# Two attention blocks on one core: when VectorE's score tiles may be issued, and how much backlog a projection step may run ahead of

## The chip, the core and the metric

The kernel runs on one core of a Trainium2 chip, as one program. The metric is the time of one execution in microseconds of device time, lower is better. A core has five engines with an instruction stream each: TensorE (in the profile PE, and PEld for its weight loads), VectorE (DVE), ScalarE (ACT), GpSimd (POOL) and SyncE (SP), which here only starts transfers. They meet through semaphores. TensorE writes its results to PSUM, which has eight banks; ScalarE and VectorE take them from there to SBUF.

## The reference

Two blocks read inputs of 2048 x 640 in bf16 and their outputs are set side by side. Block A is softmax attention with 32 heads of 20 columns, block B is linear attention with the same sizes.

```python
def _A_ref(x, wqkv, wo):                       # H = 32, Dh = 20, S = 2048
    qkv = (lambda x, *d: x.transpose(*d))((x @ wqkv).reshape(B, S, 3, H, Dh), 2, 0, 3, 1, 4)
    q, k, v = qkv[0], qkv[1], qkv[2]
    scores = jnp.einsum("bhqd,bhkd->bhqk", q, k) * (Dh ** -0.5)
    p = _softmax(scores, axis=-1)
    o = jnp.einsum("bhqk,bhkd->bhqd", p, v)
    return (lambda x, *d: x.transpose(*d))(o, 0, 2, 1, 3).reshape(B, S, D) @ wo
...
    phi = lambda t: jnp.where(t > 0, t + 1, jnp.exp(t)) + 1e-6     # block B
    pq, pk = phi(q), phi(k)
    kv = jnp.einsum("bhsd,bhse->bhde", pk, v)
    z = jnp.einsum("bhsd->bhd", pk)
    num = jnp.einsum("bhqd,bhde->bhqe", pq, kv)
    den = jnp.einsum("bhqd,bhd->bhq", pq, z)[..., None] + 1e-6
```

## The kernel before

**Work of block A.** The attention is cut into 32 groups n: four stretches of 512 queries (`qc = n // 8`), and in each of them eight groups of four heads (`g = n % 8`). A group has 16 key tiles of 128 keys, and a key tile has four score tiles, one for each head: 128 keys x 512 queries, one PSUM bank. The contraction is short, so four heads' score matmuls can stand in four row strips of TensorE at once; such a burst is called R here. All other matmuls with a narrow output (value products, projections, output projection) are issued as bursts of four column strips, called C.

**Two ways to an exponential.** Most key tiles go to ScalarE: the two score tiles of one R burst fill two banks (`SB`, banks 0 and 1 or 2 and 3), one activation takes both of them to SBUF (`exp_op`, L1740). It writes to the ring `f_PT` of 16 tiles, and four tiles that are there make one value burst. The other key tiles (`DKT` or `DSUB`, chosen by `dset`, L1556) go to VectorE. It scales and clamps one bank at a time to int16 bits of an approximate power (L1644), into one of six slots of `f_Sr`. The key tile is then used three times in a value burst, and between the uses GpSimd adds a constant to all its bits (`add_op`, L1814). So a key tile of VectorE's costs three value bursts, four VectorE instructions and two GpSimd instructions, and one of ScalarE's costs one value burst and two activations. All value bursts of a group add up in one bank, and the next group's can start only when that bank has been read (`norm`, L1818).

**Who decides the order.** The order of all instructions is written when the program is built. The class `_Fast` keeps a clock of its own for each engine with assumed costs, and whenever an engine's clock is the lowest, it picks that engine's next instruction. On the chip the instructions run in the order written, with semaphores where one needs another. For TensorE `try_pe` (L1986) asks in this order:

1. `try_burst` (L1654): the next two score tiles of ScalarE's, if their banks are free, and if Q and K for them are there (`kready`). VectorE's tiles may ride in the strips that are left, in banks 5 to 7.
2. `try_aux`, if a projection or B step has been begun (`self.cur`) and fewer than `PVHI` of ScalarE's finished tiles wait for their value bursts.
3. `try_pv` (L1758): a value burst.
4. `d_burst` (L1707): VectorE's tiles in a burst of their own, if their lead is under `DMIN`.
5. `try_aux` for a new step, and last `filler`, a matmul on zeros.

A projection or B step takes a bank of 5, 6 and 7 too, from its first burst until VectorE has read it. A VectorE tile does so as well (`take_d`, L1626); `dfl` counts those that VectorE has not started yet. The lead is `dlead` (L1649): VectorE tiles issued, less ScalarE tiles issued times the ratio of the two over the whole program. A tile of the next group can be issued ahead, as far as slots, Q and K allow. A ride is wanted if the lead is under `DLEAD` and `dfl` is under `DMAX`; a second one in the same burst if the lead is under `DOUBLE` and `dfl` is still under `DMAX`:

```python
        want = self.dlead() < self.DLEAD and self.dfl < self.DMAX
...
                if self.dlead() < self.DOUBLE and self.abank and self.dfl < self.DMAX:
```

**Order of the whole.** The first two head groups' projections come first, the others are interleaved with attention in a queue (`qa`), strictly in its order: for each chunk of heads Q, then for each of four stretches of keys K and four tiles of V. For the chunks after the first two groups the K and Q pieces go through VectorE to `f_sq` and by small transfers to their strips. Block B's steps (`qb`) start when all K and V are done. The output projection of a stretch of queries comes when its eight groups are done.

Of the kernel before, what the change touches and what calls it, by code (L numbers as in the profile page):

```python
# [750 lines left out]
class _Fast:  # L751
# [7 lines left out]
    DKT = (1, 4, 7, 10, 13)  # L759
    DSUB = (1, 4, 7, 10)  # L760
    NFULL = 4
    NEARLY = 4
    DOUBLE = 2.0
    PH = (0, 42, 89)
    WP = 0.7578125
    STEP = 20.0
    DMIN = 2
    PVHI = 9
    FILL = 0.62
    DMAX = 2  # L770
    DLEAD = 14
    SW = 107.0

    def __init__(self, nc, sch, es, ps, A_x, A_wqkv, A_wo, B_x, B_wqkv, B_wo, out):
# [781 lines left out]
    def dset(self, n):  # L1556
        return self.DKT if n >= self.NEARLY and (n * self.NFULL) % 8 < self.NFULL else self.DSUB

# [95 lines left out]
    def try_burst(self, t):  # L1654
# [18 lines left out]
        post = []  # L1673
        want = self.dlead() < self.DLEAD and self.dfl < self.DMAX
        slack = self.free["act"] - t - 560
        if want:
# [6 lines left out]
            if pd is not None:  # L1683
# [3 lines left out]
                rows.add(pd[1])  # L1687
                if self.dlead() < self.DOUBLE and self.abank and self.dfl < self.DMAX:
                    b = min(self.abank, key=lambda x: self.est("pe", (), (("ps", x),)))
# [296 lines left out]
    def try_pe(self, t):  # L1986
        if self.try_burst(t):
            return True
        if self.cur is not None and self.aexp - 4 * self.apv < self.PVHI and self.try_aux(t):
            return True  # L1990
        if self.try_pv(t):
            return True
        if self.dS < len(self.dq) and self.dlead() < self.DMIN and self.abank and self.d_burst(t):
            return True
# [200 lines left out]
```

## Time and profile before

| | |
|---|---|
| median of 3 runs | 787.47 us (787.3 to 790.4) |
| the profiled execution's own time | 787.67 us |
| its span | 785.5 us |
| TensorE matmul busy | 755.9 us, 96% |
| ScalarE busy | 707.3 us, 90% |
| VectorE busy | 617.7 us, 79% |
| GpSimd busy | 592.5 us, 75% |
| score tiles of ScalarE's | 740 activations of two |
| score tiles of VectorE's | 568 |

The profile is one execution taken by the hardware profiler. It has a page with the busy time of each engine, the costliest groups of instructions and the chain of work that ended last. Further views answer to questions: the timeline lists instructions of an engine in order with the idle time ahead of them in brackets and who ended it; the waits add these up; the table by stretches gives busy time and instruction counts (x) in chosen parts of the span. Matmuls are pipelined, so what a burst costs is read from the start of the next burst and not from its own duration. A matmul group is named by what it reads: `f_Qr,f_KT` are score tiles (one matmul for each tile), `f_PT,f_V` and `f_Sr,f_V` or `f_Sr,f_Vp` are value bursts of four, `f_xT` with a weight is a projection.

### The profile page before, as it was taken

What the parts mean: (1) busy time and instruction counts of PE and PEld (TensorE: products, weight loads), DVE (VectorE), ACT (ScalarE), POOL (GpSimd) and SP (SyncE); (2) the same over time, 40 slices, a digit from 0 to 9 for tenths busy, and PEclk for the clock granted to TensorE, in tenths of its full rate; (3) what the DMA queues carried; (4) which work ended last, traced back from release to release, by engine and by line L of the source; (5) the groups of instructions that cost most, each with busy time, mean ns of one, the idle gap of its engine ahead of it and who ended that gap; (6) DMA issues with size and microseconds to landing.
All of it is one profiled execution on the core that took longest, in us unless ns stands there. A gap on an engine that the chain in (4) does not pass through costs nothing.

```text
span 785.5 us, 25139 instructions
## 1 busy us (share of the span) xinstructions
PE 755.9 (96%) x10960; PEld 266.4 (34%) x10960; DVE 617.7 (79%) x1186; ACT 707.3 (90%) x796; POOL 592.5 (75%) x341
## 2 busy tenths in 40 slices
PE   5999999999989999999999999999999999999996
PEld 2433453234223233333333333323333333233333
DVE  4666759676986778878878787889987798889876
ACT  3479679997999999999999999989999999999990
POOL 6646655787779887787879878777987878787971
PEclk9999999999999999999999999999999999999999
DMA  9000010010520000010200000111000020000002
GB/s 307 17 3 19 19 26 21 22 29 20 129 44 23 23 11 8 14 34 7 40 2 25 30 10 9 50 47 40 23 18 17 33 53 26 20 14 31 6 2 72
DMA packets 38495, 26.34 MB, mean 34 GB/s; under 512 B 21356, under 2 KB 38380, under 8 KB 38380
## 3 DMA queue, kind: packets, MB, share of 16 engines
q1 hardware_dynamic: 35100, 21.81, 10.2%
q10 hardware_dynamic: 3280, 2.87, 1.2%
q8 instruction: 88, 1.44, 0.8%
q14 instruction: 27, 0.22, 0.1%
HBM read 9.58 MB, written 5.24 MB: 19 GB/s over the span
## 4 chain that ended last, share of the span: by engine, by line
PE 53%; ACT 34%; DVE 10%; DMA 1%; issue 1%; SPq 0%; ACTq 0%; DVEq 0%
PE ps L155 53%; ACT f_PT L1740 32%; DVE f_Sr L1644 5%; ACT ps L1277 2%; DMA f_ar<-in_A_wqkv_dram 1%; PE ps L941 1%; DVE f_ar L1387 1%; DMA f_KT<-f_sq 0%; DVE f_T L1840 0%; DVE f_ar L1308 0%; DVE f_OTn L1837 0%; DVE f_ar L1311 0%; DVE f_sq L1158 0%; DVE f_ar L1279 0%; DVE f_sq L1161 0%
## 5 line engine op out<-in xcount | busy, mean ns | idle before, releaser
L1740 ACT ACTIVATE f_PT<-ps 128x1024 bf16<-128x1024 f32 x740 | 694.5, 1101 | 53.4 <-PE ps L155 51.5
L1814 POOL TENSOR_SCALAR f_Sr<-f_Sr 128x2048 int16<-128x2048 int16 x284 | 539.1, 1898 | 134.5 <-PE ps L155 101.7
L1644 DVE TENSOR_SCALAR f_Sr<-ps 128x512 int16<-128x512 f32 x568 | 378.8, 683 | 72.3 <-PE ps L155 68.0
L155 PE MATMUL ps<-f_Qr,f_KT 32*128 32x512 bf16 x2048 | 304.6, 386 | 8.0 <-ACT f_PT L1740 2.9
L155 PEld LDWEIGHTS ps<-f_Qr,f_KT 32*128 32x128 bf16 x2048 | 76.8, 91 | 256.4 <-ACT f_PT L1740 218.7
L155 PE MATMUL ps<-f_ar 128*32 128x320 bf16 (+3 forms) x2496 | 152.1, 311 | 2.8 <-DVE f_Sr L1644 1.0
L155 PE MATMUL ps<-f_PT,f_V 128*21 128x512 bf16 x1480 | 140.2, 384 | 0.0
L155 PE MATMUL ps<-f_Sr,f_V 128*21 128x512 bf16 x1136 | 104.9, 385 | 0.6 <-DVE f_T L1840 0.4
L155 PEld LDWEIGHTS ps<-f_ar 128*32 128x32 bf16 (+1 forms) x2496 | 60.1, 96 | 70.6 <-issue 38.8
L1833 POOL TENSOR_TENSOR f_T<-f_T,f_Rt 128x512 bf16<-128x512 f32 x32 | 33.5, 1048 | 34.6 <-DVE f_Rt L1831 27.0
L155 PE MATMUL ps<-f_Sr,f_Vp 128*21 128x512 bf16 x568 | 56.6, 385 | 0.0
L155 PEld LDWEIGHTS ps<-f_PT,f_V 128*21 128x21 bf16 x1480 | 35.8, 90 | 45.9 <-issue 36.4
L155 PE MATMUL ps<-f_ar,f_xT 128*32 128x160 bf16 x1280 | 36.4, 239 | 1.5 <-DVE f_Sr L1644 0.9
L155 PEld LDWEIGHTS ps<-f_Sr,f_V 128*21 128x21 bf16 x1136 | 26.5, 90 | 33.1 <-issue 21.7
L1279 DVE SCALAR_TENSOR_TENSOR f_ar<-ps,f_ar 128x320 bf16<-128x320 f32 (+1 forms) x52 | 29.2, 562 | 10.3 <-ACT ps L1277 9.6
L155 PE MATMUL ps<-f_xT,f_ar 128*32 128x512 bf16 x480 | 36.8, 393 | 0.2
L1275 DVE TENSOR_SCALAR f_ar<-ps 128x320 f32<-128x320 f32 (+1 forms) x52 | 29.0, 558 | 5.3 <-PE ps L155 5.1
L1190 DVE CAST f_V<-ps 128x160 bf16<-128x160 f32 x64 | 19.6, 317 | 16.9 <-PE ps L155 16.1
L1277 ACT ACTIVATE ps<-ps 128x320 f32<-128x320 f32 (+1 forms) x52 | 32.1, 617 | 0.0
L155 PEld LDWEIGHTS ps<-f_ar,f_xT 128*32 128x32 bf16 x1280 | 24.5, 98 | 17.2 <-issue 7.0
L155 PE MATMUL ps<-f_wo,f_OTd 120*32 120x320 bf16 x512 | 28.5, 302 | 0.2 <-DVE f_Sr L1644 0.2
L155 PE MATMUL ps<-f_xT,f_wq 128*32 128x512 bf16 (+1 forms) x320 | 25.2, 384 | 0.7 <-DVE f_Sr L1644 0.6
(76 smaller groups left out, 360.4 us busy)
## 6 DMA issues: line engine op xcount, KB each, us to landing
out_dram<-f_st SPq DMA_DIRECT2D x32, 160.0 KB
f_ar<-in_B_wqkv_dram SPq DMA_DIRECT2D x3, 800.0 KB
f_ar<-in_A_x_dram SPq DMA_DIRECT2D x3, 640.0 KB
f_OTd<-f_OTn SPq DMA_DIRECT2D x96, 20.0 KB
f_Qr<-f_sq SPq DMA_DIRECT2D x96, 20.0 KB
f_KT<-f_sq SPq DMA_DIRECT2D x96, 20.0 KB
f_ar<-in_A_wqkv_dram ACTq DMA_DIRECT2D x2, 800.0 KB
f_wq<-in_A_wqkv_dram ACTq DMA_DIRECT2D x1, 800.0 KB
```

What stands on the lines that cost most here:

```text
L155: lambda e: e.matmul(out, lhsT, rhs, start=start, stop=stop, tile_position=tp, skip_group_check=sgc),
L941: self.sch.op("pe", lambda e, m=m: e.transpose(m["out"], m["in"], m["id"]), reads=m["reads"], writes=m["writes"], inc=m.get("inc", k == le ...
L1190: self.push("dve", lambda e: e.tensor_copy(dst, src), (("ps", b), "Vones"), (("V", t, r),), _c_dve(w), prio=1, after=None if isd else last)
L1275: self.push("dve", lambda e: e.tensor_scalar(r1, src, 0.0, 1e-6, op0=ALU.max, op1=ALU.add), (("ps", b),), (rk,), _c_dve(n), prio=1, ok=ok, ...
L1277: "act", lambda e: e.activation(src, src, AF.Exp), (), (("ps", b),), _c_act(n), prio=0,
L1279: "dve", lambda e: e.scalar_tensor_tensor(dst, src, 1.0, r1, op0=ALU.min, op1=ALU.add),
L1387: self.push("dve", lambda e: e.tensor_tensor(self.kvm[:, c, 0:21 * nh], acc, self.mask[:, c, 0:21 * nh], op=ALU.mult), (("kva", c), ("mask ...
L1644: post = lambda: self.push("dve", lambda e: e.tensor_scalar(self.Sr[:, s, i, :], self.ps[:, b, :], 0.0, 32639.0 - self.PH[-1], op0=ALU.max ...
L1740: return _Op("act", lambda e: e.activation(self.PT[:, s0:s0 + n, :], ps[:, b0:b0 + n, :], AF.Exp, scale=math.log(2.0) / 128.0, bias=self.l ...
L1814: return e.tensor_scalar(v, v, inc, 1.0, op0=ALU.add, op1=ALU.mult)
L1833: self.nmul, lambda e: e.tensor_tensor(T2v, Tv, R.unsqueeze(2).broadcast_to([128, 16, 32]), op=ALU.mult),
```

## The change

Six constants of the class `_Fast`, and nothing else.

```diff
     NFULL = 4
-    NEARLY = 4
-    DOUBLE = 2.0
+    NEARLY = 8
+    DOUBLE = 6.0
     PH = (0, 42, 89)
     WP = 0.7578125
     STEP = 20.0
-    DMIN = 2
-    PVHI = 9
+    DMIN = -6
+    PVHI = 13
     FILL = 0.62
-    DMAX = 2
-    DLEAD = 14
+    DMAX = 1
+    DLEAD = 8
     SW = 107.0
```

`NEARLY` is the first group from which even groups give VectorE five key tiles instead of four. With 8 in the place of 4, groups 4 and 6 have four. `DMAX` 1 lets a tile ride only when none of VectorE's is in flight. Since `dfl` is one after the first ride, the second ride in a burst, which `DOUBLE` governs, doesn't occur any more. `DLEAD` 8 stops rides at a lead of eight tiles instead of 14. `DMIN` -6 allows bursts of VectorE's tiles alone only when they are more than six behind, where before it was as soon as the lead was under two. `PVHI` 13 lets a begun projection or B step go ahead of value bursts until 13 of ScalarE's tiles wait, instead of nine.

## The prediction

> **What bounds the kernel now.** I read the page first, for the busy shares, and its groups for the size of each kind of work.
>
> ```profile
> span 785.5 us, 25139 instructions
> PE 755.9 (96%) x10960; PEld 266.4 (34%) x10960; DVE 617.7 (79%) x1186; ACT 707.3 (90%) x796; POOL 592.5 (75%) x341
> ```
> ```profile
> L1740 ACT ACTIVATE f_PT<-ps 128x1024 bf16<-128x1024 f32 x740 | 694.5, 1101 | 53.4 <-PE ps L155 51.5
> L1814 POOL TENSOR_SCALAR f_Sr<-f_Sr 128x2048 int16<-128x2048 int16 x284 | 539.1, 1898 | 134.5 <-PE ps L155 101.7
> L1644 DVE TENSOR_SCALAR f_Sr<-ps 128x512 int16<-128x512 f32 x568 | 378.8, 683 | 72.3 <-PE ps L155 68.0
> ```
>
> TensorE and ScalarE are both nearly full over the span, so I asked for stretches. The table of busy time, cut at 60, 200 and 760 us:
>
> ```profile
> 60.00:200.00 140.00, 136.74 (x2278) 52.16 (x2275) 99.63 (x198) 118.05 (x128) 96.31 (x53) 1.00 0.09 23
> 200.00:760.00 560.00, 549.11 (x7551) 182.56 (x7547) 468.81 (x872) 552.27 (x630) 454.11 (x256) 1.00 0.11 27
> ```
>
> The first pair in a row is TensorE, the fourth ScalarE. TensorE is 98% busy in both. ScalarE is 99% busy after 200 us (552.27 of 560), and 84% between 60 and 200 (118.05 of 140). So ScalarE sets the pace late, and TensorE, which then does the projections besides, sets it early. ScalarE's waits say the same, asked for 60 to 205 us and then for 200 to 765:
>
> ```profile
> ACT f_PT L1740 <- PE ps L155: 21.9, 13, 4.7
> ```
> ```profile
> ACT f_PT L1740 <- PE ps L155: 5.9, 11, 1.2
> ```
>
> 21.9 us of waiting in 13 waits, against 5.9 us in a stretch four times as long. Where the early ones lie, from ScalarE's timeline:
>
> ```profile
> 87.41 1.02 ACT L1740 ACTIVATE f_PT<-ps 128x1024 bf16<-128x1024 f32 x1 [4.69 <-PE ps L155]
> ...
> 117.85 1.02 ACT L1740 ACTIVATE f_PT<-ps 128x1024 bf16<-128x1024 f32 x1 [3.42 <-PE ps L155]
> 120.67 43.46 ACT L1740 ACTIVATE f_PT<-ps 128x1024 bf16<-128x1024 f32 x47 [1.80 <-PE ps L155]
> 165.72 6.52 ACT L1740 ACTIVATE f_PT<-ps 128x1024 bf16<-128x1024 f32 x7 [1.59 <-PE ps L155]
> ...
> 194.28 1.03 ACT L1740 ACTIVATE f_PT<-ps 128x1024 bf16<-128x1024 f32 x1 [3.49 <-PE ps L155]
> 196.95 3.77 ACT L1740 ACTIVATE f_PT<-ps 128x1024 bf16<-128x1024 f32 x4 [1.64 <-PE ps L155]
> ```
>
> The activations overlap: 47 take 43.46 us, so one costs (43.46 - 1.10) / 46 = 0.92 us of ScalarE, and not the 1101 ns of its row. The waits lie where K of the next head chunk is still being projected. In such a place every burst that TensorE spends on something else delays ScalarE.
>
> **What the change removes: bursts of VectorE's tiles alone.** Three rows for 60 to 200 us, of the table asked for ScalarE's line, for VectorE's line and for the score matmuls alone (the tile f_KT; its first pair is TensorE):
>
> ```profile
> 60.00:200.00 140.00, 118.05 (x128) 1.00 0.09 23
> ```
> ```profile
> 60.00:200.00 140.00, 62.90 (x98) 1.00 0.09 23
> ```
> ```profile
> 60.00:200.00 140.00, 58.58 (x354) 15.34 (x351) 0.73 (x1) 0.00 (x0) 1.00 0.09 23
> ```
>
> 354 score tiles are ScalarE's 128 pairs and some 98 of VectorE's. How these 98 were issued I took from the order of bursts in the program of before, laid on the trace's matmuls one by one. In this stretch 44 tiles ride, and 53 stand in 41 bursts of their own. The whole program has 55 such bursts with 72 tiles, seven of them ahead of 60 us and only three after 212 us. The cause is the old DMIN: the lead in that order stays between -8.6 and +2.4 here, so nearly always under 2, and under -6 only in parts of the time from 107 to 125 us. With -6 most of these bursts have no leave any more.
>
> What one costs is read from TensorE's timeline:
>
> ```profile
> 117.82 0.39 PE L155 MATMUL ps<-f_Sr,f_Vp 128*21 128x512 bf16 x4
> 118.14 0.39 PE L155 MATMUL ps<-f_Qr,f_KT 32*128 32x512 bf16 x2
> 118.46 0.53 PE L155 MATMUL ps<-f_ar,f_xT 128*32 128x160 bf16 x20
> 119.32 0.53 PE L155 MATMUL ps<-f_ar,f_xT 128*32 128x160 bf16 x20 [0.33 <-DVE f_Sr L1644]
> ...
> 121.75 0.60 PE L155 MATMUL ps<-f_Qr,f_KT 32*128 32x512 bf16 x4
> 122.28 0.40 PE L155 MATMUL ps<-f_PT,f_V 128*21 128x512 bf16 x4
> 123.04 0.39 PE L155 MATMUL ps<-f_Qr,f_KT 32*128 32x512 bf16 x2
> 123.36 0.32 PE L155 MATMUL ps<-f_ar,f_xT 128*32 128x160 bf16 x8
> ```
>
> The pair at 118.14 is VectorE's alone between C bursts. The next burst starts 0.32 us later, as after ScalarE's own burst at 123.04. At 121.75 a pair alone and ScalarE's pair follow each other, and this takes 0.53 us, 0.21 more than one burst. So a burst is 0.21 us, and a change between R and C about 0.11. Alone next to ScalarE's burst costs 0.21, alone between C bursts 0.21 + 2 x 0.11 = 0.43. By their neighbours in the order 40 of the 55 are of the first kind: a mean of (40 x 0.21 + 15 x 0.43) / 55 = 0.27 us, for 41 bursts 11.1 us. The Trainium skill ("TensorEngine Tiling (Array Packing)", Key Properties) says that changing the tiling mode drains TensorE. The 0.11 us agrees, but the trace charges it only where the burst brings a change of its own; were two drains due for each, the sum would be 41 x 0.43 = 17.6 us.
>
> Not all of them go. In 127 of ScalarE's bursts of this stretch 41 carried a ride. 41 didn't because K or Q of VectorE's next tile was missing, 26 for want of a bank or with two in flight, 19 because the tiles left were in occupied strips. The first reason goes when VectorE's tiles fall behind ScalarE's, whose K is there; the second goes in part, since bursts alone no longer take up to three banks at once. I take two rides in three bursts, 85 tiles. Needed are 98, less the six or so that NEARLY takes away by then, less five that are put off as the lead settles lower: 87. An estimate of up to eight bursts alone stays, and 33 x 0.27 = 8.9 us of TensorE are free. A ride costs TensorE nothing that a row shows: the burst of two at 123.04 and the one of three at 596.59 (below) have the same 0.39 us. Not every free 0.1 us reaches ScalarE, since the trace shows TensorE waiting at times too (0.33 us at 119.32, for a bank that VectorE's tile held). I take two thirds: **-6 us**, bounds 0 and -11.1. The end at 0 holds if the projections wait for something else.
>
> **Banks.** The wait at 119.32 is a projection's for a bank. With at most one ride in flight such waits get rarer. I take **-1.5 us**, bounds 0 and -4, the latter about one wait of 0.33 us for each of 13 stalls. A gain in place of these waits is all that is claimed here; VectorE's 683 ns for each tile stay.
>
> **NEARLY.** Groups 4 and 6 give ScalarE two key tiles more: 8 tiles, 4 activations, 4 x 0.92 = 3.7 us. VectorE loses 8 x 683 ns and GpSimd 4 x 1898 ns, on neither of which the end hangs there. TensorE loses 4 value bursts (4 x 0.21 = 0.8 us) and gains 4 R bursts with their changes (4 x 0.43 = 1.7 us). The groups lie at about 141 to 164 and 186 to 212 us in the order laid on the trace, with 1.59, 3.49 and 1.64 us of waits of ScalarE in the rows above. Half hides there: **+1.9 us**, bounds 0 and +3.7. If the waits go by the terms above, the cover is gone and it is 3.7.
>
> **Precedence of begun steps.** With nine to twelve ScalarE tiles waiting, a begun step now goes first. In the order of before 66 value bursts, 16 of them between 100 and 200 us, were issued ahead of a begun step in that state. A step has at most five or six bursts, of 0.21 us or less. Queued behind it are the value bursts, and behind those the free places of the ring of 16: with 12 waiting, ScalarE can still do two activations, 1.8 us. So it mostly stays covered. Where a group ends, the next group's value bursts wait for the shared bank anyhow and the ring fills; 5.9 us of ScalarE's late waits are of that size. I take **+0.6 us**; bounds -2 (projections early by 16 x 0.12) and +5 (those late waits nearly doubled).
>
> **DMAX, DOUBLE, DLEAD late.** In the order of before 23 of the 438 rides after 200 us started with one tile in flight, one in 19, and six second rides exist in all. After the change 560 tiles come on 744 activations, 0.753 a burst. Between 300 and 760 us, 361 of 473 bursts carried one, 0.763, and some were held only by slots. Less one in 19, that leaves 0.72 to 0.76: the lead stays about level, between -6 and +5 instead of the +4 to +11 of before, and few bursts alone come back. What that does to a group's end is the second rival; on the likely path it is 0.
>
> **The tail.** It needs four rows, of ScalarE and TensorE:
>
> ```profile
> 742.25 24.24 ACT L1740 ACTIVATE f_PT<-ps 128x1024 bf16<-128x1024 f32 x26
> ```
> ```profile
> 771.79 3.24 PE L155 MATMUL ps<-f_wo,f_OTn 128*32 128x320 bf16 x32 [0.99 <-DVE f_ar L1476]
> 774.97 2.74 PE L155 MATMUL ps<-f_ar 128*32 128x320 bf16 x60
> 779.57 1.54 PE L155 MATMUL ps<-f_ar 128*32 128x320 bf16 x40 [0.61 <-DVE f_ar L1499]
> ```
>
> The activations end at 766.5, and B's last projections still run after A's. VectorE's last tiles may come up to 6 later, but B's rest (774.97 to 781) fills the wait: 0, bounds 0 and +3.
>
> **Sum.** -6 - 1.5 + 1.9 + 0.6 = -5.0 us. The profiled execution's own time of 787.67 us (span 785.5) becomes 782.7; it lies 0.2 us over the median of 787.47, so the forecast is 782.5 us. A measurement of this kernel can tell about 0.5% from no change, 3.9 us.
>
> **Rivals.** *No change.* The early waits could be the projections' own round trip and not TensorE's share. The chain of waits has both:
>
> ```profile
> 136.48 21.22 PE ps L155 x235
> ...
> 169.51 1.90 DMA f_KT<-f_sq
> ```
>
> For it speaks the transfer of K in the second row, against it the first: long stretches of pure TensorE. Then the first term is 0, and -1.5 + 1.9 + 0.6 = +1 us gives 788.5. Its upper form: ScalarE's emptying of PSUM binds everywhere, and only the 3.7 us count, 791.2. The Trainium skill ("TensorEngine Tiling (Array Packing)", PSUM Bottleneck) warns that packing speeds up TensorE and not the emptying of PSUM, and the rows after 200 us agree. Also here: the lead sinks below -6 at once, and as many bursts alone remain as before.
>
> *Slower: VectorE's tiles come too late for the end of their group.* Even groups keep GpSimd busy without a gap, and the group's bank is read after its last addition:
>
> ```profile
> 594.56 19.69 POOL L1814 TENSOR_SCALAR f_Sr<-f_Sr 128x2048 int16<-128x2048 int16 x10
> ```
> ```profile
> 596.59 0.39 PE L155 MATMUL ps<-f_Qr,f_KT 32*128 32x512 bf16 x3
> ```
> ```profile
> 615.54 0.72 DVE L1840 STREAM_TRANSPOSE f_T<-ps 128x512 f32<-128x512 f32 x1 [0.43 <-PE ps L155]
> ```
>
> The last tile of this group (24) was scored at 596.59. It needs two additions, 3.8 us, a value burst between and VectorE's 0.7: it could come as late as about 608, 11 us later, without harm. A tile of lead is worth 0.92 x 740 / 568 = 1.2 us. The order has a lead of 9 here, so it is used up at about 0. At -4, four tiles further, each end of an even group comes 4 x 1.2 = 4.8 us late, the ring of ScalarE is then full, and in three such groups (26, 28, 30) this costs 14 us: 787.5 - 5 + 14 = 796.5. It decides when the lead stays below 0 after some 640 us. For it speaks that the early stretch leaves the lead near -6; against it that the rides hold level and that groups up to 20 have the global ratio's slack.
>
> *Slower: the ring.* The precedence costs its +5 and the rest its means: 787.
>
> **How the numbers follow.** The forecast, faster by over 0.5%: 0.54. No change with its upper form, and the ring: 0.30. Late tiles: 0.16. Summed bounds are 787.5 - 11.1 - 4 - 2 = 770 and, with the late tiles, 796.5 and a little over. The range leaves about a tenth at each side: 772 to 796; the likely case alone has 774 to 783.5. Faster 0.54, same 0.30, slower 0.16.
>
> **What would show it.** Right: ScalarE's waits between 60 and 205 us fall from 21.9 to some 14 us; 744 activations, 560 tiles on VectorE, 280 additions; score bursts of one tile nearly gone from TensorE's timeline. Wrong: waits after 200 us well over 5.9 us, GpSimd idle inside the ten additions of an even group, or the early waits unchanged with few bursts alone.

## The result and the profile after

The changed kernel takes 769.09 us (median of 4 runs, 767.51 to 771.32) against 788.93 us for the kernel before on the same chip (787.3 to 791.74): a ratio of 0.9747, 95% interval 0.9705 to 0.9788. The profiled execution took 769.45 us with a span of 767.3. The forecast was 782.5 us in a range of 772 to 796: the side is right, the time lies under the range, and the gain is about four times the 5 us foretold.

From the page of the changed kernel, the busy times and the three groups that the prediction quoted:

```profile
span 767.3 us, 25089 instructions
...
PE 740.2 (96%) x10936; PEld 259.4 (34%) x10936; DVE 613.4 (80%) x1178; ACT 709.1 (92%) x800; POOL 585.7 (76%) x337
...
L1740 ACT ACTIVATE f_PT<-ps 128x1024 bf16<-128x1024 f32 x744 | 696.7, 1123 | 37.8 <-PE ps L155 37.6
...
L1814 POOL TENSOR_SCALAR f_Sr<-f_Sr 128x2048 int16<-128x2048 int16 x280 | 532.3, 1901 | 130.7 <-PE ps L155 90.8
L1644 DVE TENSOR_SCALAR f_Sr<-ps 128x512 int16<-128x512 f32 x560 | 380.7, 684 | 83.9 <-PE ps L155 76.2
```

TensorE is 15.7 us less busy and ScalarE 1.8 us more. ScalarE's idle time ahead of its activations fell from 53.4 to 37.8 us, although it does four activations more. VectorE's tiles waited a little longer (83.9 us for 72.3), GpSimd's additions about as long.

The table by stretches of the changed kernel (TensorE first, ScalarE fourth), and under it two answers of ScalarE's waits, for 60 to 205 us and for 200 to 745 us (in total, times, longest):

```profile
60.00:200.00 140.00, 137.41 (x2311) 48.20 (x2309) 113.35 (x217) 132.51 (x145) 103.29 (x60) 1.00 0.20 45
```
```profile
ACT f_PT L1740 <- PE ps L155: 7.5, 3, 4.6
```
```profile
ACT f_PT L1740 <- PE ps L155: 8.4, 12, 1.6
```

TensorE was full before and is full now (136.74 and 137.41 us of 140), but ScalarE gets 145 activations out of this stretch instead of 128. ScalarE's early waits fell from 21.9 to 7.5 us; the prediction looked for some 14. Where the rest lie, from ScalarE's timeline:

```profile
58.48 22.20 ACT L1740 ACTIVATE f_PT<-ps 128x1024 bf16<-128x1024 f32 x24 [4.93 <-PE ps L155]
85.33 22.14 ACT L1740 ACTIVATE f_PT<-ps 128x1024 bf16<-128x1024 f32 x24 [4.65 <-PE ps L155]
109.70 23.09 ACT L1740 ACTIVATE f_PT<-ps 128x1024 bf16<-128x1024 f32 x25 [2.23 <-PE ps L155]
133.41 82.61 ACT L1740 ACTIVATE f_PT<-ps 128x1024 bf16<-128x1024 f32 x90 [0.62 <-PE ps L155]
```

These waits are of another kind. The short runs with 3.42 to 4.69 us of waiting ahead of one activation, where K was missing, are gone. The waits at 58, 85 and 110 us are 24 activations apart, each of them one ring (eight activations) behind the end of group 0, 1 or 2. The ring is full there until the last value bursts of the group, which are VectorE's tiles, are done and its bank has been read. From 133 us on ScalarE runs through to the end of this view.

How far ScalarE is at 200 us is the best measure for what follows. The activations begun up to there and behind, from the table asked for ScalarE's line, first before, then after:

```profile
0.00:200.00 200.00, 145.84 (x157) 1.00 0.16 48
200.00:800.00 600.00, 548.69 (x584) 0.99 0.11 28
```
```profile
0.00:200.00 200.00, 163.89 (x178) 1.00 0.25 64
200.00:800.00 600.00, 532.84 (x567) 0.99 0.08 23
```

At 200 us 740 - 157 = 583 activations were left, and now 744 - 178 = 566: 17 fewer, 17 x 0.92 = 15.6 us. (It began 21 more, four of them ahead of 60 us, and it has four more to do.) The last activation ends at 752.2 us instead of 766.5, 14.3 earlier, so 1.3 us were given back on the way. The tail behind it is 15.1 us instead of 19.0, 3.9 less. The sum, -15.6 + 1.3 - 3.9 = -18.2 us, is the difference of the spans. Block B began earlier: its first activation (L1277) stands at 222.9 us instead of 285.7. That this shortened the tail isn't shown: in the run with NEARLY 4 below it stands at 269.4 us, and the tail is 15.8 us.

By the program's order laid on the trace, TensorE's bursts from 14 to 200 us, without the fillers, were 158 of ScalarE's score pairs, 160 value bursts, 524 of projections and 48 of VectorE's tiles alone: 890. After the change they are 177, 178, 535 and 1: 891. It is an exchange, burst for burst.

### The profile page after: what moved, and what is told of

It reads as the page before. It is cut to its first block, busy times and chain, and to the rows that moved or that the text cites. A ratio compares the mean times of both kernels' runs of the same rounds, so it can differ in the third digit from the quotient of the medians.

```text
span 767.3 us, 25089 instructions
## 1 busy us (share of the span) xinstructions
PE 740.2 (96%) x10936; PEld 259.4 (34%) x10936; DVE 613.4 (80%) x1178; ACT 709.1 (92%) x800; POOL 585.7 (76%) x337
## 4 chain that ended last, share of the span: by engine, by line
PE 46%; ACT 45%; DVE 6%; SPq 1%; issue 1%; ACTq 1%; DMA 0%; POOL 0%; DVEq 0%
PE ps L155 45%; ACT f_PT L1740 43%; ACT ps L1277 2%; DVE f_Sr L1644 2%; PE ps L941 1%; SPq L1155 1%; DVE f_ar L1387 0%; DVE f_xT L1074 0%; DVE f_st L1244 0%; DVE f_T L1840 0%; DVE f_KT L1098 0%; DVE f_OTn L1837 0%; POOL f_Sr L1814 0%; DMA f_KT<-f_sq 0%; DMA f_Qr<-f_sq 0%
## 5 line engine op out<-in xcount | busy, mean ns | idle before, releaser
L1740 ACT ACTIVATE f_PT<-ps 128x1024 bf16<-128x1024 f32 x744 | 696.7, 1123 | 37.8 <-PE ps L155 37.6
L1814 POOL TENSOR_SCALAR f_Sr<-f_Sr 128x2048 int16<-128x2048 int16 x280 | 532.3, 1901 | 130.7 <-PE ps L155 90.8
L1644 DVE TENSOR_SCALAR f_Sr<-ps 128x512 int16<-128x512 f32 x560 | 380.7, 684 | 83.9 <-PE ps L155 76.2
L155 PE MATMUL ps<-f_Qr,f_KT 32*128 32x512 bf16 x2048 | 295.2, 386 | 9.0 <-ACT f_PT L1740 3.8
L155 PEld LDWEIGHTS ps<-f_Qr,f_KT 32*128 32x128 bf16 x2048 | 73.9, 91 | 254.6 <-ACT f_PT L1740 230.4
L155 PE MATMUL ps<-f_ar,f_xT 128*32 128x160 bf16 x1280 | 34.1, 234 | 0.1
L1277 ACT ACTIVATE ps<-ps 128x320 f32<-128x320 f32 (+1 forms) x52 | 32.5, 626 | 0.1
L1837 DVE STREAM_TRANSPOSE f_OTn<-f_T 128x512 bf16<-128x512 bf16 x32 | 22.5, 703 | 2.3 <-POOL f_T L1833 1.9
```

The source lines that it names most:

```text
L155: lambda e: e.matmul(out, lhsT, rhs, start=start, stop=stop, tile_position=tp, skip_group_check=sgc),
L1277: "act", lambda e: e.activation(src, src, AF.Exp), (), (("ps", b),), _c_act(n), prio=0,
L1644: post = lambda: self.push("dve", lambda e: e.tensor_scalar(self.Sr[:, s, i, :], self.ps[:, b, :], 0.0, 32639.0 - self.PH[-1], op0=ALU.max ...
L1740: return _Op("act", lambda e: e.activation(self.PT[:, s0:s0 + n, :], ps[:, b0:b0 + n, :], AF.Exp, scale=math.log(2.0) / 128.0, bias=self.l ...
L1814: return e.tensor_scalar(v, v, inc, 1.0, op0=ALU.add, op1=ALU.mult)
L1837: "dve", lambda e: e.transpose(self.OTn[:, o, :], self.T2[:]), ("T2",), (("OTn", o),),
```

## The experiments

All ratios are to the kernel before. A cost over the changed kernel is the difference of two ratios times 788 us, good to about 4 us. "Activations by 200 us" are counted as above; bursts alone are counted in the order laid on the trace. In the expectations A is the theory that the gain is TensorE's time of the bursts alone, B and later E that it is banks held by VectorE's tiles, C that it is the precedence of begun steps, and D that late tiles of VectorE's cost the time at the ends of groups. Beside the constants each order also has its own number of zero matmuls (fillers); the other work is that of the kernel that it varies. In three of these orders (DMIN alone, DMAX alone, and DMIN 2 in the changed kernel) a tile of block A's output takes a slot of the buffer `f_st` that one of block B's still holds, so that a part of the output is wrong. Their times stand for an order of the same work, not for a kernel to use.

### Parts of the change, alone and together

The leave for bursts alone, in the kernel before:

```diff
-    DMIN = 2
+    DMIN = -6
```

> The kernel before with DMIN -6 alone; its order has 7 bursts of VectorE's tiles alone instead of 55. Theory A (the gain is TensorE time of the bursts alone): 48 x 0.27 = 13 us less, near 776. Theory B (bursts alone and second rides hold banks and VectorE, and projection steps wait for these): more than A's 13 us where banks get free, but second rides stay, so 770 to 778 and the stretch ahead of 60 us little better. Theory C (the precedence of begun steps makes the gain): within 5 us of before, 784 or more.

Measured: 784.22 us, ratio 0.9949 (0.9924 to 0.9974). By its time alone it is C's, 784 us or more, and too slow for A and B. But up to 200 us it does what A and B say. All activations up to there, and those from 60 us on:

```profile
0.00:200.00 200.00, 155.62 (x168) 0.99 0.24 63
60.00:200.00 140.00, 122.35 (x133) 0.99 0.19 45
```

168 activations instead of 157 are 10.1 us by 200 us, five of them behind 60 us (133 for 128). The bursts alone up to 200 us fell from 48 to 7. But the last activation ends only 2.8 us earlier than before. So 7.3 us were lost again behind 200 us. ScalarE's waits from 200 to 760 us are about that much longer, 14.2 us where the same view of the kernel before has 5.9 and 1.2:

```profile
ACT f_PT L1740 <- PE ps L155: 10.7, 13, 2.5
ACT f_PT L1740 <- DVE f_ar L1387: 1.8, 1, 1.8
ACT ps L1277 <- DVE f_ar L1275: 1.7, 1, 1.7
```

Four of these waits, 6.4 us together, stand at 207, 252, 615 and 659 us, each one ring behind the end of group 6, 8, 24 or 26. These are groups in which VectorE has five key tiles. Another place, from TensorE's timeline, with the table of 494 to 518 us:

```profile
498.59 0.40 PE L155 MATMUL ps<-f_PT,f_V 128*21 128x512 bf16 x4
500.78 0.39 PE L155 MATMUL ps<-f_zt 128*32 128x256 bf16 x1 [1.79 <-DVE f_Sr L1644]
501.11 0.61 PE L155 MATMUL ps<-f_Qr,f_KT 32*128 32x512 bf16 x3
```
```profile
494.00:498.00 4.00, 4.00 (x49) 1.23 (x46) 4.00 (x9) 3.88 (x5) 3.08 (x3) 1.00 0.12 30
498.00:501.00 3.00, 1.03 (x9) 0.30 (x8) 2.96 (x5) 1.18 (x3) 2.92 (x2) 0.90 0.58 161
501.00:514.00 13.00, 13.00 (x85) 2.86 (x88) 7.05 (x11) 9.86 (x11) 12.18 (x7) 0.50 0.31 97
514.00:518.00 4.00, 4.00 (x56) 1.00 (x56) 3.34 (x6) 3.90 (x5) 0.02 (x1) 0.99 0.00 0
```

A filler waits 1.79 us for a bank that one of VectorE's tiles holds, and everything behind it on TensorE waits too. The granted clock (third from the right) then stays at 0.50 for 13 us, in which ScalarE is busy for 9.86 us only. The same in small stands at 185 us: a score burst waits 0.72 us for VectorE's tile, and the clock is 0.57 from 186 to 190 us. But the clock doesn't explain why this kernel is slow. The profiled execution is the slowest of its ten (786.92 us, mean clock 0.989). The other nine had 0.995 to 1.000, and the two with 1.000 took 783.6 and 782.85 us, hardly less than the median.

Fewer bursts alone and one more change, at most one of VectorE's tiles in flight:

```diff
-    DMIN = 2
+    DMIN = -6
...
-    DMAX = 2
+    DMAX = 1
```

> The kernel before with DMIN -6 and DMAX 1; 4 bursts alone, no second rides. A: the same as with DMIN alone, near 776. B: better than with DMIN alone by 3 us or more, and near the changed kernel, 768 to 773. C: 784 or more.

Measured: 767.78 us, ratio 0.9747 (0.9707 to 0.9787): the whole gain with two of the six constants. That is B's expectation (768 to 773 us) and some 8 us under A's, so more is in it than TensorE's time.

```profile
0.00:200.00 200.00, 160.58 (x174) 1.00 0.24 64
200.00:800.00 600.00, 532.97 (x567) 1.00 0.08 23
60.00:200.00 140.00, 129.25 (x141) 1.00 0.19 45
```
```profile
ACT f_PT L1740 <- PE ps L155: 4.6, 6, 1.4
```

Over the run with DMIN alone it has 6 activations more by 200 us (5.5 us), and 8 more between 60 and 200 us (141 for 133). Its last activation gains 11.4 us more behind 200 us, where its waits (the second view, 200 to 760 us) are 4.6 us instead of 14.2, and its tail is 1.8 us shorter. These spans differ by 18.7 us, the ratios by 16. All four executions of it had a clock of 0.999 or 1.000 and took at most 768.69 us, so at least 14 us lie between the two kernels at an equal clock of 1.000. C is out: PVHI is 9 here. That the limit does this by itself was the next question:

```diff
-    DMAX = 2
+    DMAX = 1
```

> The kernel before with DMAX 1 alone: 56 bursts alone in its order (13 ahead of 60 us, 38 to 200 us), no ride beside a tile in flight instead of 38. Theory A: 785 to 791 us, since the bursts alone stay. Theory E, if the rides beside a tile in flight do their harm by themselves: 773 to 781 us; if bursts alone, which hold up to three banks whatever DMAX is, take their place: 785 us and over.

Measured: 796.35 us, ratio 1.0101 (1.0059 to 1.0143). Alone it is slower: 56 bursts alone remain, which take up to three banks whatever DMAX is, and 159 activations come by 200 us. The last one ends at 764.0 us, but the tail behind it is 27.4 us instead of 19.0. So the parts don't add up: -4 and +8 us alone, -20 us together. The other side, in the changed kernel:

```diff
-    DOUBLE = 6.0
+    DOUBLE = 2.0
...
-    DMAX = 1
+    DMAX = 2
```

> The changed kernel with DMAX 2 and DOUBLE 2 again: no burst alone in its order, but 88 of its 744 score bursts carry a ride while another VectorE tile is still in flight, 60 of them two at once. Theory A (the gain is TensorE's time of the bursts alone): 767 to 773 us. Theory E (a second VectorE tile in flight holds a bank that the projections and block B's steps wait for, early and late): 778 to 787 us, with TensorE's waits between 60 and 200 us and ScalarE's waits after 200 us up.

Measured: 778.96 us, ratio 0.9877 (0.9842 to 0.9913), 10 us over the changed kernel, as E expected. Only two activations of it are lost by 200 us (176); 5.66 us are a single wait at the end of group 30:

```profile
743.20 3.77 ACT L1740 ACTIVATE f_PT<-ps 128x1024 bf16<-128x1024 f32 x4 [5.66 <-PE ps L155]
```

### What the last free bank is worth

In the kernel before, a burst alone is let out only if a second bank is free, and leaves that one:

```diff
+            if self.jS < len(self.groups) and len(self.abank) < 2:
+                break
...
-        if self.dS < len(self.dq) and self.dlead() < self.DMIN and self.abank and self.d_burst(t):
+        if self.dS < len(self.dq) and self.dlead() < self.DMIN and len(self.abank) >= 2 and self.d_burst(t):
```

> The kernel before, where a burst alone now leaves one of the three shared banks free: 56 bursts alone in its order (9 ahead of 60 us, 41 to 200 us), 49 rides beside a tile in flight. Theory A (TensorE's time of the bursts alone): 785 to 790 us. Theory E (it is the last free bank that a burst alone takes from a projection): 775 to 782 us.

Measured: 783.78 us, ratio 0.9931 (0.9906 to 0.9957), between the two expectations. 56 bursts alone are still there, and 162 activations come by 200 us instead of 157. So about 5 us of the harm of bursts alone are banks, if the rest of the order, which is planned anew, counts for nothing, and TensorE's time isn't all of it.

### What a microsecond of TensorE is worth

The changed kernel's own order, with 69 bursts of zeros added behind value bursts, first between 60 and 200 us, then behind 300 us:

```diff
+        elif 60000.0 <= self.now < 200000.0 and self.ntax < 80 and self.pvcnt % 2 == 0:
+            self.ntax += 1
+            for k in range(2):
+                self.sch.mm(self.ps[0:21, b, 256 * k:256 * k + 256], self.zt[:, 0:21], self.zt[:], start=False,
+                            stop=False, reads=("zt",), writes=(("ps", b),), tp=(0, 0), inc=(k == 1))
```

> The changed kernel's own order, with 69 more bursts of two matmuls of zeros (256 columns each) between 60 and 200 us of the builder's clock, each right behind a value burst and of its form and bank: about 0.2 us of TensorE each, 14 us together, and no bank, VectorE tile or transfer. Theory A (in this stretch a microsecond of TensorE is a microsecond of the end): 780 to 785 us, and some 12 to 15 activations fewer by 200 us. Theory B (the early stretch waits for banks, VectorE's tiles and the projections' round trip): 770 to 776 us.

Measured: 779.82 us, ratio 0.9883 (0.9854 to 0.9912): 10.7 us for 69 x 0.21 = 14.5 us of TensorE, or 0.74 for each microsecond (0.5 to 1.0 by the uncertainty), a little under A's range.

```profile
60.00:200.00 140.00, 139.57 (x2335) 56.18 (x2333) 106.37 (x201) 127.93 (x134) 97.10 (x55) 1.00 0.18 43
```

2.2 us were taken from TensorE's idle time (137.41 before them, 139.57 with them), and 11 activations are missing here (134 for 145), 10.1 us.

```diff
+        elif 300000.0 <= self.now < 700000.0 and self.ntax < 69 and self.pvcnt % 5 == 0:
```

> The same 69 bursts of zeros, spread behind 300 us of the builder's clock instead. Theory A (ScalarE sets the pace after 200 us, so TensorE's time is covered there): 769 to 774 us, the tail behind the last activation longer by a few us at most. If TensorE's time is as scarce here as before 200 us, so that block B's steps run over the end: 780 to 785 us.

Measured: 774.44 us, ratio 0.9827 (0.9798 to 0.9857): 6.3 us, 0.43 for each microsecond. Late time of TensorE is cheaper than early time, but the result lies just over A's upper end: it isn't covered by ScalarE altogether. The last of this kind has the zeros in the row form (32 rows instead of 128), between 60 and 200 us again:

```diff
-                self.sch.mm(self.ps[0:21, b, 256 * k:256 * k + 256], self.zt[:, 0:21], self.zt[:], start=False,
+                self.sch.mm(self.ps[0:21, b, 256 * k:256 * k + 256], self.zt[0:32, 0:21], self.zt[0:32, :], start=False,
```

> The run with 69 bursts of zeros between 60 and 200 us again, but each burst in the score matmuls' row tiling (32 rows) behind a value burst (128 rows), so that each brings two changes of form more or less, as a burst alone between value bursts does. That run cost 10.7 us over the changed kernel, 0.15 a burst: 0.71 of its 0.21 us of TensorE. Theory A with the prediction's price of a change (0.11 us, so 0.43 us a burst): 0.71 x 69 x 0.43 = 21 us, 788 to 792 us. If a change of form costs nothing where TensorE waits anyway: 779 to 782 us.

Measured: 789.97 us, ratio 0.9999 (0.9961 to 1.0037): 20 us, as A expected, where the same columns without a change of form cost 10.7. First the run in the value bursts' form, then this one, from TensorE's timeline:

```profile
120.63 0.39 PE L155 MATMUL ps<-f_Sr,f_Vp 128*21 128x512 bf16 x4
120.85 0.38 PE L155 MATMUL ps<-f_zt 128*21 128x256 bf16 x2
121.16 0.39 PE L155 MATMUL ps<-f_Qr,f_KT 32*128 32x512 bf16 x3
```
```profile
120.24 0.39 PE L155 MATMUL ps<-f_PT,f_V 128*21 128x512 bf16 x4
120.55 0.38 PE L155 MATMUL ps<-f_zt 32*21 32x256 bf16 x2
120.87 0.39 PE L155 MATMUL ps<-f_Qr,f_KT 32*128 32x512 bf16 x3
```

In the same form the zeros follow after 0.22 us, in the other after 0.31. The score burst behind them comes 0.31 and 0.32 us later, so going from these zeros to the score form is a change as well. Ahead of a score burst, then, the row form adds only one change and not the two that the expectation counted for each. Some 42 of the 69 stand so in the trace, and the expectation's working then gives about 18 us in the place of 21. The 20 us agree with both within their uncertainty. The Trainium skill ("TensorEngine Tiling (Array Packing)", Key Properties) says that a change of tiling mode drains TensorE, and these rows agree, at about 0.1 us for each.

### How many bursts alone

The changed kernel with other values of DMIN:

```diff
-    DMIN = -6
+    DMIN = 2
```

> The changed kernel with DMIN 2 as before; its order has 151 bursts alone. A: 148 x 0.27 = 40 us more, near 809. B: more than 40 us early in the program, over 810. C: within 10 us of the changed kernel.

Measured: 808.3 us, ratio 1.0272 (1.0221 to 1.0322), A's figure. Its order has 151 bursts alone; 41 us for 148 more are 0.28 us each. It has 161 activations by 200 us, and block B runs 37.0 us over the last activation.

```diff
-    DMIN = -6
+    DMIN = -2
```

> The changed kernel with DMIN -2: 45 bursts alone in its order (3 ahead of 60 us, 20 to 200 us, 22 to 400 us), against 3 with -6 and 151 with +2. Theory A by stretch: 22 early ones more at 0.27 x 0.71 = 0.19 us and some 20 later ones at a third of that: 773 to 776 us. If each burst alone costs what it did on the mean with +2 (39.2 us for 148 bursts, 0.26 us): 779 to 782 us.

Measured: 781.83 us, ratio 0.991 (0.9878 to 0.9942): 13 us for 42 bursts more, or 0.31 us each, as the mean price has it and not A's price by stretch. By 200 us only 3 activations are missing (175), 2.8 us. The rest came late, and 4.46 us of it in one wait, again at the end of group 30:

```profile
744.64 14.77 ACT L1740 ACTIVATE f_PT<-ps 128x1024 bf16<-128x1024 f32 x16 [4.46 <-PE ps L155]
```

So a price for each burst alone holds up to 200 us only; what they do to the late order is a matter of where VectorE stands at a group's end.

### The precedence, and the ends of late groups

The changed kernel with the old precedence:

```diff
-    PVHI = 13
+    PVHI = 9
```

> The changed kernel with PVHI 9 as before; 11 bursts alone. A and B: within 4 us of the changed kernel, 766 to 773, since the precedence was priced at +0.6. C: 780 or more.

Measured: 791.77 us, ratio 1.0047 (1.0017 to 1.0077), what C expected, and slower than before. But C needs a loss in the early stretch, and 177 activations came by 200 us, for 178. The loss comes behind: 9 activations fewer than in the changed kernel have begun by 550 us, and 22 fewer by 700 us. From ScalarE's timeline:

```profile
616.35 4.69 ACT L1740 ACTIVATE f_PT<-ps 128x1024 bf16<-128x1024 f32 x5 [2.57 <-PE ps L155]
...
693.16 20.27 ACT L1740 ACTIVATE f_PT<-ps 128x1024 bf16<-128x1024 f32 x22 [4.16 <-PE ps L155]
717.64 42.27 ACT L1740 ACTIVATE f_PT<-ps 128x1024 bf16<-128x1024 f32 x46 [4.22 <-PE ps L155]
```

In the order VectorE's lead is about -3 on the mean from 550 to 700 us of the planner's clock, where the changed kernel has +3 and then +7. The waits shown stand one ring behind the ends of groups 24, 27 and 28: the ring of 16 is full. That is the prediction's second rival, in another kernel. Its test keeps PVHI 9 and gives the lead back, by bursts alone that are allowed at -3 late:

```diff
-    PVHI = 13
+    PVHI = 9
...
-        if self.dS < len(self.dq) and self.dlead() < self.DMIN and self.abank and self.d_burst(t):
+        if self.dS < len(self.dq) and self.dlead() < (-6 if t < 300000 else -3) and self.abank and self.d_burst(t):
```

> The changed kernel with PVHI 9 again and DMIN -6 up to 300 us of the builder's clock, -3 behind it. Its order has 6 bursts alone, and VectorE's lead in the late groups stays near +3 tiles, where the run with PVHI 9 alone had -2 to -5 and took 791.8 us. Theory D (the 22 us of that run came from VectorE's late tiles, the mechanism of the second rival): 766 to 774 us, ScalarE's waits after 550 us under 8 us instead of 24. Theory C (the precedence of begun steps is what makes the gain): 786 to 794 us, and the early activations as late as in the kernel before.

Measured: 771.79 us, ratio 0.9787 (0.9743 to 0.9832), as D expected. It has two bursts alone behind 200 us of the planner's clock, and the 20 us are gone. ScalarE's waits between 550 and 780 us (in total, times, longest), with PVHI 9 alone and with the lead given back:

```profile
ACT f_PT L1740 <- PE ps L155: 17.0, 8, 4.2
```
```profile
ACT f_PT L1740 <- PE ps L155: 4.6, 3, 2.5
```

Why the order with PVHI 9 holds its lead lower isn't shown. The precedence alone, in the kernel before:

```diff
-    PVHI = 9
+    PVHI = 13
```

> The kernel before with the precedence alone (PVHI 13): 61 bursts alone in its order. The prediction priced the precedence at +0.6 us (-2 to +5): by that 785 to 792 us. Theory C (the precedence by itself makes a good part of the gain): 783 us or less.

Measured: 795.32 us, ratio 1.0087 (1.0056 to 1.0119): 7 us slower, a little over the prediction's bound of 5. By 200 us it is 4 activations ahead (161), and late it loses more than that. C is out from this side too.

The groups with a tile fewer for VectorE, undone in the changed kernel:

```diff
-    NEARLY = 8
+    NEARLY = 4
```

> The changed kernel with NEARLY 4 again: 740 activations instead of 744, two more tiles of VectorE in each of groups 4 and 6 on either side. The prediction priced NEARLY 8 at +1.9 us (0 to +3.7), because four activations come to ScalarE: by that 765 to 769 us. If the groups 4 and 6 end late by VectorE's tiles (rides alone do not bring 10 tiles in time while the lead is near -6): 770 to 776 us, with ScalarE's waits up at the ends of groups 4 and 6.

Measured: 776.29 us, ratio 0.9848 (0.9822 to 0.9875): 8 us slower, though it has four activations fewer. The second expectation holds in place and nearly in time; at the ends of groups 4, 5 and 6 ScalarE waits:

```profile
152.74 22.45 ACT L1740 ACTIVATE f_PT<-ps 128x1024 bf16<-128x1024 f32 x24 [1.92 <-PE ps L155]
176.44 20.27 ACT L1740 ACTIVATE f_PT<-ps 128x1024 bf16<-128x1024 f32 x22 [1.25 <-PE ps L155]
199.67 21.19 ACT L1740 ACTIVATE f_PT<-ps 128x1024 bf16<-128x1024 f32 x23 [2.96 <-PE ps L155]
```

But the run with DMIN and DMAX alone has NEARLY 4 as well and is as fast as the changed kernel. So NEARLY 8 doesn't make the gain; beside PVHI 13 and DLEAD 8 it keeps it. DLEAD alone was not tried. No version here is faster than the changed kernel beyond the uncertainty: 767.78 us with two constants has the same ratio.

## Why the prediction was right and wrong

**Which engine sets the pace early** was right. TensorE's zeros between 60 and 200 us cost 0.74 us at the end for each microsecond; the prediction had taken "two thirds". Its unit prices, 0.21 us a burst and 0.11 a change of form, also stand by the rows: 0.22 us to the next burst in the same form, 0.31 in the other.

**Bursts alone, -6 us (0 to -11.1).** Measured with DMIN alone by 200 us: -10.1 us, within the bounds. The step "Not all of them go" counted too few: 33 of 41, and the stretch ahead of 60 us was left out. In the changed kernel 3 of 55 are left. Up to 200 us 41 fewer in the run with DMIN alone give 41 x 0.27 x 0.74 = 8.2 us of the 10.1. By parts this fits less well: ahead of 60 us seven fewer give 1.4 us, and six activations (5.5 us) were gained; behind it 34 fewer give 6.8 us, and five (4.6 us) were. So the sum agrees partly by luck. That their harm isn't TensorE's time alone is what the run that leaves one bank free says, too.

**Banks, -1.5 us (0 to -4), and "DMAX, DOUBLE, DLEAD late": 0.** This is the step that failed most: the limit of one tile in flight was priced at 1.5 us in all. With DMIN at -6 it is worth 16 us by the ratios; by the profiles 5.5 us up to 200 us and 13.2 us behind (11.4 and a tail of 1.8), of which some 3 us belong to the one execution of DMIN alone that was profiled. The prediction counted only waits of projections for a bank, 0.33 us each, between 60 and 200 us. There the limit brings ScalarE 8 activations, 7.4 us, more than DMIN alone brings there (5). 1.5 us of it are idle time of TensorE (135.80 us busy from 60 to 200 us with DMIN alone, 137.31 with both) and some 1.7 us, in that execution, the clock at 186 to 190 us; the rest isn't assigned. Late it was put at nothing, and ScalarE's waits from 200 to 760 us fell from 14.2 to 4.6 us. Of what went, 6.4 us stood behind the ends of four groups, and some 5 us of ScalarE's idle time stood at 498 to 514 us, with the halved clock of that execution. Undone in the changed kernel, the limit costs 10 us, more than half of it in one wait. So it is worth 10 to 16 us by the two comparisons, by more than one way, and not by a fixed price.

**NEARLY, +1.9 us (0 to +3.7).** As work this was right: four activations more are among the 744. As an effect it has the wrong sign in the changed kernel, -8 us, because the waits at the ends of groups 4 to 6, which the prediction said hide half of it, are what it removes.

**Precedence, +0.6 us (-2 to +5).** Alone it is +7 us. In the changed kernel its removal costs 24 us, and with the late lead given back some 3, which these runs can hardly tell from nothing. It was priced as if a constant had one price.

**The tail, 0 (0 to +3).** It is 3.9 us shorter, outside the bounds. The step that failed is that it could only get longer: "B's rest fills the wait" took B's rest as given, and block B started 63 us earlier here. Whether that is the reason stays open.

**The rivals.** *No change* is out. *VectorE's tiles come too late* didn't decide in the changed kernel, where the lead in the order is +2 on the mean from 400 us on and +6 from 600 us on, but it is real: 17 us of waits with PVHI 9, 5.66 with DMAX 2, 4.46 with DMIN -2. The signs named for it are there in a small way. ScalarE's waits behind 200 us rose from 5.9 us to 8.4, and GpSimd is idle ahead of the last addition of group 24:

```profile
583.32 17.77 POOL L1814 TENSOR_SCALAR f_Sr<-f_Sr 128x2048 int16<-128x2048 int16 x9
603.64 1.90 POOL L1814 TENSOR_SCALAR f_Sr<-f_Sr 128x2048 int16<-128x2048 int16 x1 [2.56 <-PE ps L155]
```

*The ring*, as a price of the precedence, is seen in the kernel before alone (+7 us). In the changed kernel the ring is full early, at 58, 85 and 110 us, and for another reason, the ends of groups.

**What stays open.** The 18 us are placed: 15.6 by 200 us, 3.9 in the tail, 1.3 given back. Two constants make them, and by 200 us they have the whole 15.6 (174 activations for 157), 10.1 with DMIN and 5.5 more with DMAX. How these divide between TensorE's time and the banks can't be settled by these runs, since each constant also changes the order that the others meet. Nor is it shown what holds up the ends of four groups with DMIN alone, where the lead in the order is positive.

## What to carry to other kernels

Where an engine is full in a stretch, count its instructions by kind before and after: what goes is exchanged burst for burst for what is waiting, and the time at the end follows the engine that gets these. Price a resource that is held, such as a bank, by what queues in order behind the one who waits for it, and not by the wait itself. Before a stretch of one profile is made the cause, ask whether the other executions had it: here the halved clock of one execution explains some 3 us of 16. And where a planner writes the order, test constants in pairs: here parts that cost -4 and +8 us alone give -20 us together.

## What the runs showed of the hardware

The granted clock of TensorE fell to half after some short idle times. In the run with DMIN alone TensorE was busy for 1.03 of 3 us (498 to 501), and was then at 0.50 for 13 us although it was busy for all 13.00 of them. In the changed kernel itself:

```profile
461.00:464.00 3.00, 2.28 (x22) 0.49 (x21) 2.97 (x7) 1.97 (x2) 0.82 (x1) 0.87 0.58 174
464.00:470.00 6.00, 6.00 (x42) 1.12 (x40) 3.22 (x7) 4.34 (x6) 2.96 (x3) 0.50 0.44 140
470.00:476.00 6.00, 5.90 (x65) 1.72 (x65) 4.48 (x8) 6.00 (x7) 5.76 (x4) 1.00 0.05 14
```

Here 0.72 us of idle time in 3 us were followed by 6 us at 0.50, and ScalarE was busy for 4.34 of them. The Trainium skill ("TensorE: Matmul & The Clock Gate", Part 1) gives about 3.4 us as the window, of idleness to fall to half and of sustained work to come back. The falls came here with much less idle time, and one lasted 13 us of work; the measurement decides. But idle time of this size doesn't always bring a fall. In the run with NEARLY 4 TensorE waited 1.30 us at 487.6 us, again for a bank that VectorE's tile held, and the clock stayed:

```profile
487.00:490.00 3.00, 1.70 (x18) 0.48 (x15) 2.82 (x5) 1.77 (x3) 2.84 (x3) 1.00 0.42 96
490.00:493.00 3.00, 2.96 (x33) 0.99 (x30) 2.73 (x6) 3.00 (x4) 2.92 (x2) 1.00 0.82 269
```

What decides between the two isn't shown. The clock differs between executions of one kernel, too: with PVHI 13 in the kernel before the mean clock was 0.980 in the execution of 798.97 us and 0.992 in the one of 791.05. A mean clock of 0.99 for an execution, as in the profile of the changed kernel, hides such a stretch.
